# A planner that judges orders by an in-order replay with late transfers: one fused attention and feed-forward kernel

## The chip, the cores and the metric

The kernel runs on one core of a Trainium2 chip. A core has five engines that each execute their own queue of instructions in order: TensorE (PE, matmuls and their weight loads), VectorE (DVE), ScalarE (ACT), GpSimd (POOL) and SyncE (SP), which here only issues DMA transfers. They wait for each other through semaphores. The metric is the device time of the program in microseconds (us); the median of three runs is compared.

## What is computed

A linear attention over 8 batches, 8 heads, 576 positions and 64 dimensions per head, followed by a feed-forward layer over all 4608 tokens (512 to 2048 to 512) in float32:

```python
q_s = q - np.max(q, axis=-1, keepdims=True)
q_s = np.exp(q_s)
q_s = q_s / (np.sum(q_s, axis=-1, keepdims=True) + 1e-09)
k_s = k - np.max(k, axis=2, keepdims=True)
k_s = np.exp(k_s)
k_s = k_s / (np.sum(k_s, axis=2, keepdims=True) + 1e-09)
kv = np.einsum('bhsd,bhse->bhde', k_s, v)
attn = np.einsum('bhsd,bhde->bhse', q_s, kv).astype(np.float32)
...
x = np.ascontiguousarray(attn.transpose(0, 2, 1, 3)).reshape(B * S, H * D)
h = x @ w_in
g = np.where(h >= 1, h, np.where(h <= -1, 0.0, (h + 1) ** 2 / 4.0))
out = (g @ w_out).astype(np.float32)
```

## The kernel before

*Tiling.* The 4608 tokens are cut into nine chunks of 512. A float32 operand is held as two parts (high and low), and a product of two such operands takes three matmuls of 128 x 128 by 512. The first three chunks go one by one: for each of 16 blocks of 128 hidden features there is a first layer (`first_layer`, L1613, tile h), the activation g on ScalarE and VectorE (`middle`), and a second layer into four PSUM banks (`second_layer`, L1822, tile o). The other six chunks go in pairs, three turns: `two_first_layers` (L1671) takes seven products for four blocks (tiles hA, hB, hC, with VectorE additions at L1695 and copies sn), and half of the g blocks of the second chunk are kept in DRAM (`keep`) and read back (`recall`, tile gs). The weights are split on the chip during the first chunk (`weights`, L455 to L497: loads st, shift L467, join L470, split), stored to DRAM and streamed in later (`fetch`, L535, tiles w from b or s). The attention of a chunk (`attention`, `attention_two`, L1215 and after) is spread over the feed-forward work of the chunk before: loads of k, v and q (L1240), a maximum over k (L1252), exponentials, the kv product (L1304), the maximum and sum over q, the product x (L1491), its copy to DRAM (xk, L1527) and back (xc, L1161). A finished output bank is copied by ScalarE or VectorE to osb (L392, L394) and stored (L1880).

*What sets the order.* None of these steps is issued where it stands in the code. Each is an `Op` of a `Plan`, with its engine (sometimes two to choose from), a price in us, a due time, its dependencies (data and the freeing of buffers, by `Ring`), its kilobytes if it is a transfer, and whether it locks the port that VectorE and GpSimd share. `Plan.order` builds a first order by due times. `Plan.settle` then repeats 450 times: `late` (places every step as late as it can, from the end), a random shift of up to eight steps that aren't transfers, near an idle place of PE in the plan, and `early` (places every step as early as it can). A try is kept if the planned end doesn't grow. At the end the steps of all engines are issued sorted by planned start, and that order is each engine's queue.

*How transfers are planned.* A transfer takes 0.45 us of SyncE, then `FIRST` us, then its kilobytes at `KB_PER_US` on a "wire". `early` and `late` put it into any free hole of the SyncE row and of the wire row (`gap`), whatever was placed there before. `save` and `read`, for what the kernel writes to DRAM itself, add a margin of 1.2 us; loads of the inputs (k, v, q, st) and the stores of the output are plain `op`s with a margin of 0.

Of the kernel before, what the change touches and what calls it, by code (L numbers as in the profile page):

```python
# [73 lines left out]
LATE = 8  # L74


START, STEP, LEAD = 24.0, 5.5, 20.0


class Op:  # L80
# [4 lines left out]
    def __init__(self, engine, us, due, emit, deps, port, kb, slack, other=()):  # L85
        self.engine, self.us, self.due, self.emit = engine, us, due, emit
        self.port, self.kb, self.slack = port, kb, slack
        self.ways = ((engine, us, port), *other)
        self.deps, self.users = deps, []
        self.missing = len(deps)  # L90
        self.ready = self.after = 0.0
        self.store = False
        self.margin = 0.0
        for d in deps:
            d.users.append(self)

# [18 lines left out]
class Plan:  # L115
# [1 line left out]

    HOP, FIRST, KB_PER_US = 0.12, 2.6, 310.0  # L120

    UNDER_WAY = 8

    TURNS = 450

    PATIENCE = 0.2

# [24 lines left out]
    def save(self, us, due, emit, deps, kb):  # L152
        op = self.op("SP", us, due, emit, deps, kb=kb)
        op.store = True
        op.margin = self.MARGIN
        return op

    def read(self, us, due, emit, deps, kb):
# [38 lines left out]
    def late(self, order):  # L197

        end = max(op.end for op in order)
        used = {e: [] for e in ("PE", "ACT", "DVE", "POOL", "SP", "port", "wire")}  # L200
        starts = {}
        for op in sorted(order, key=lambda op: (op.start, op.end), reverse=True):
            at = issue = end
            for u in op.users:
                if u.engine == op.engine == "SP" and not op.store:
                    issue = min(issue, starts[u] - 0.45)
                else:
                    at = min(at, starts[u] - self.hop(op, u))
            if op.kb:
                us = op.kb / self.KB_PER_US  # L210
                at = self.gap([used["wire"]], us, at - us - op.margin, True) - self.FIRST
                starts[op] = self.gap([used["SP"]], 0.45, min(at, issue), True)
            else:
                starts[op] = self.fit(op, at - op.us, used, True)
        return starts

    def early(self, starts):

        used = {e: [] for e in ("PE", "ACT", "DVE", "POOL", "SP", "port", "wire")}
        for op in self.ops:  # L220
            op.missing = len(op.deps)
        ready = [(starts[op], op.n, op) for op in self.ops if not op.missing]
        heapify(ready)
        while ready:
            op = heappop(ready)[2]
            for u in op.users:
                u.missing -= 1
                if not u.missing:
                    heappush(ready, (starts[u], u.n, u))
            at = op.after  # L230
            for d in op.deps:
                if d.engine == op.engine == "SP" and not d.store:
                    at = max(at, d.start + 0.45)
                else:
                    at = max(at, d.end + self.hop(d, op))
            if op.kb:
                us = op.kb / self.KB_PER_US
                op.start = self.gap([used["SP"]], 0.45, at)
                op.end = self.gap([used["wire"]], us, op.start + self.FIRST) + us + op.margin
            else:  # L240
                op.start = self.fit(op, at, used, False)
                op.end = op.start + op.us
        return sorted(self.ops, key=lambda op: (op.start, starts[op], op.n))

    def settle(self):


        order, rng = self.order(), random.Random(1)
        for i in range(self.TURNS):
            was = max(op.end for op in order)  # L250
            kept = [(op, op.start, op.end) for op in order]
            starts = self.late(order)
            if i > 1:
                pe = sorted((o.start, o.end) for o in order if o.engine == "PE")
                idle = [(b[0], b[0] - a[1]) for a, b in zip(pe, pe[1:]) if b[0] > a[1] + 0.05]
                about = rng.choices([x for x, _ in idle], [x for _, x in idle])[0]
                about -= rng.uniform(0.0, 8.0)
                near = [o for o in self.ops if o.engine != "SP" and abs(o.start - about) < 6]
                for o in rng.sample(near, min(len(near), rng.choice((1, 2, 4, 8)))):
                    starts[o] += rng.gauss(0.0, 3.0)  # L260
                order = self.early(starts)
                starts = self.late(order)
            order = self.early(starts)
            if max(op.end for op in order) > was + 1e-9:
                for op, op.start, op.end in kept:
                    pass
                order = [k[0] for k in kept]
        return order

    def bias(self, op, engine):  # L270
# [9 lines left out]
    def order(self):  # L280
        self.inherit()
        free = {op.engine: 0.0 for op in self.ops}
        avail = {e: [] for e in free}
        port = wire = 0.0
# [10 lines left out]
        while len(out) < len(self.ops):  # L295
# [32 lines left out]
            if locks:  # L328
                port = end
            if op.kb:  # L330
                end = wire = max(t + self.FIRST, wire) + op.kb / self.KB_PER_US
                landed.append(end)
                end += op.margin
            op.end = end
# [11 lines left out]
def tile_linear_attention_then_ffn(  # L346
# [321 lines left out]
    def attention(c, pr, due, step, slack, kdue=None):  # L668
# [318 lines left out]
        if has_k:  # L987
            if c < KT:
# [7 lines left out]
                rzs.free(kz)  # L996
                rrz.take(kz)
                et = room(f"ps h{pr % 2}", 1) if first else rpk
                tr = do("PE", 0.7, 2, kt_tr, ke, *rpk.wait(), *(et.wait() * first))
                rpk.take(tr)  # L1000
                copies = [("DVE", 0.69, False)], [("ACT", 0.25, False)]
                kc = do("ACT", 0.58, 2.5, kt_copy, tr, *rk.wait(), other=copies[0])
# [62 lines left out]
        qn = do("POOL", 1.04, 3, q_rows("qrz", ALU.mult), qz, port=True)  # L1065
        rqz.free(qn)
        if first:
            tr = do("PE", 0.6, 3.6, q_tr, qn, *rpq.wait())
        elif rows:
            mm = do("PE", 0.95, 3.6, kv_mm, kc, kd, lv, *rpk.wait())  # L1070
            rpk.take(mm)
            rk.free(mm)
            kh = do("ACT", 0.62, 4.2, kv_hi, kz, mm, *parts)
            kl = do("DVE", 0.57, 4.4, kv_lo, kh)
            rpk.free(kl)
            tr = do("PE", 0.6, 3.6, q_tr, qn, *rpq.wait())
        else:
            rqt = room("wk qt", 1)
            tr = do("DVE", 0.71, 3.6, q_blocks, qn, *rqt.wait(), port=True)
            rqt.take(tr)  # L1080
# [134 lines left out]
    def attention_two(c, h, kdue, qdue):  # L1215
# [131 lines left out]
        if c < NB:  # L1347
# [8 lines left out]
                    pr, "v", v[c, pr], [P, KJ, P + 2], 325, kdue + 33 + 3 * i, "v"  # L1356
                )
            for i, pr in enumerate(two):
                km = do("DVE", 0.8, kdue + 6 * i, k_max(i), loads[pr, "k"], *maxed, port=True)
                maxed = [km]  # L1360
                if not i:
                    rm.take(km)
                loads[pr, "m"] = km
# [24 lines left out]
            ra = ring("ps a", 1)  # L1388
            at = kdue + 34
            deps = [loads[pr, "v"] for pr in two]  # L1390
            mm = do("PE", 1.68, at, kv_mms, *exps, *deps, *ra.wait())
            ra.take(mm)
            for pr in two:
                rooms[pr, "k"].free(mm)
# [162 lines left out]
        for i, pr in enumerate(two):  # L1557
# [8 lines left out]
            rql.take(lo)  # L1566
            rqt.free(lo)
            deps = [kvdone.get((c - 1, pr)), kvdone.get((c, pr))]
            xm = do("PE", 0.9, at + 5, x_mm(pr), lo, *[d for d in deps if d], *ra.wait())
            ra.take(xm)  # L1570
            rqh.free(xm)
            rql.free(xm)
# [481 lines left out]
```

## Time and profile before

| | |
|---|---|
| median of three runs | 861.32 us (857.89, 861.32, 863.23) |
| the profiled execution | 863.48 us, of which the span from the first to the last instruction is 861.70 us |
| PE matmuls | 840.2 us busy, 4272 instructions |
| DVE, ACT, POOL | 512.6, 473.5, 301.0 us busy |
| DMA | 166.39 MB in 455 transfers of SyncE, 193 GB/s in the mean |
| longest waits of PE | 3.8, 3.7 and 3.2 us |

Matmuls are pipelined: one of 512 columns is shown with some 390 ns but the next starts after about 227, so the busy time of PE is the union of overlapping pieces, not their sum. A granted clock (PEclk) below 1.00 says that PE ran at half speed for a part of that stretch. In a row of a timeline, what stands in brackets is how long the engine was idle before it and what ended the idle time. The engine named as the end of a wait is the last link: it may itself have stood behind something in its queue.

### The profile page before, as it was taken

What the parts mean: (1) busy time and instruction counts of PE and PEld (TensorE: products, weight loads), DVE (VectorE), ACT (ScalarE), POOL (GpSimd) and SP (SyncE); (2) the same over time, 40 slices, a digit from 0 to 9 for tenths busy, and PEclk for the clock granted to TensorE, in tenths of its full rate; (3) what the DMA queues carried; (4) which work ended last, traced back from release to release, by engine and by line L of the source; (5) the groups of instructions that cost most, each with busy time, mean ns of one, the idle gap of its engine ahead of it and who ended that gap; (6) DMA issues with size and microseconds to landing.
All of it is one profiled execution on the core that took longest, in us unless ns stands there. A gap on an engine that the chain in (4) does not pass through costs nothing. (4 is left out here: it accounts for less than half of the span.)

```text
span 861.7 us, 12255 instructions
## 1 busy us (share of the span) xinstructions
PE 840.2 (97%) x4272; PEld 685.7 (80%) x4272; DVE 512.6 (59%) x956; ACT 473.5 (55%) x834; POOL 301.0 (35%) x270
## 2 busy tenths in 40 slices
PE   8799999999999999999898999999999999999998
PEld 6587788888888887878676888888887888888786
DVE  7887867767766747767577626677652034545300
ACT  7787856455655656555466345556574344445522
POOL 5554565542557253111213162122155810000153
PEclk9999999999999999999999999999999999999999
DMA  8788975257476548557566525566456244544232
GB/s 331 246 295 301 301 243 183 88 196 256 158 273 232 192 150 333 182 179 262 183 195 220 167 92 189 171 218 214 156 170 218 88 152 141 172 159 147 71 113 86
DMA packets 65582, 166.39 MB, mean 193 GB/s; under 512 B 7280, under 2 KB 7536, under 8 KB 65520
## 3 DMA queue, kind: packets, MB, share of 16 engines
q1 hardware_dynamic: 65520, 165.61, 56.9%
q8 instruction: 34, 0.56, 0.3%
q14 instruction: 28, 0.23, 0.1%
HBM read 122.06 MB, written 43.52 MB: 192 GB/s over the span
## 5 line engine op out<-in xcount | busy, mean ns | idle before, releaser
L1822 PE MATMUL o<-wl,gh 128*128 128x512 f32 x576 | 228.3, 396 | 4.0 <-ACT osb L392 3.5
L1822 PE MATMUL o<-wh,gl 128*128 128x512 f32 x576 | 226.0, 392 | 0.1
L1822 PE MATMUL o<-wh,gh 128*128 128x512 f32 x576 | 225.5, 391 | 0.0
L1671 PE MATMUL hA<-x,w 128*128 128x512 f32 x576 | 148.5, 394 | 5.0 <-DVE c L1695 4.8
L1671 PEld LDWEIGHTS hA<-x,w 128*128 128x128 f32 x576 | 107.8, 189 | 29.9 <-DVE c L1695 7.0
L1822 PEld LDWEIGHTS o<-wl,gh 128*128 128x128 f32 x576 | 108.8, 189 | 27.9 <-ACT osb L392 4.8
L1822 PEld LDWEIGHTS o<-wh,gl 128*128 128x128 f32 x576 | 108.8, 189 | 24.9 <-POOL gl L1811 0.9
L1822 PEld LDWEIGHTS o<-wh,gh 128*128 128x128 f32 x576 | 109.1, 189 | 21.6
L1613 PE MATMUL h<-x,w 128*128 128x512 f32 x432 | 110.5, 400 | 5.8 <-DVE gl L1811 4.6
L1613 PEld LDWEIGHTS h<-x,w 128*128 128x128 f32 x432 | 80.7, 190 | 24.6 <-DVE gl L1811 5.2
L1765 ACT ACTIVATE r<-r 128x512 f32<-128x512 f32 x144 | 90.9, 632 | 3.6
L1671 PE MATMUL hC<-x,w 128*128 128x512 f32 x288 | 73.7, 391 | 0.3 <-DVE gl L1811 0.2
L1762 ACT ACTIVATE r<-c,half 128x512 f32<-128x512 f32 x48 | 34.7, 722 | 65.0 <-DVE c L1695 64.7
L1806 ACT CAST gh<-gs 128x512 fp32r<-128x512 f32 x42 | 26.1, 622 | 73.7 <-PE o L1822 62.9
L1671 PEld LDWEIGHTS hC<-x,w 128*128 128x128 f32 x288 | 53.7, 188 | 12.6 <-ACT sn_P L392 0.8
L1436 POOL TENSOR_TENSOR q<-q,qmb 128x512 f32<-128x512 f32 x28 | 30.2, 1097 | 94.1 <-DVE qmb L1428 73.1
L1811 POOL TENSOR_TENSOR gl<-gs,gh 128x512 fp32r<-128x512 f32 x34 | 43.8, 1293 | 49.2 <-ACT gh L1806 49.1
L1762 ACT ACTIVATE r<-h,half 128x512 f32<-128x512 f32 x48 | 32.9, 688 | 47.8 <-PE h L1613 47.6
L1436 POOL TENSOR_TENSOR q<-q,qzb 128x512 f32<-128x512 f32 x28 | 29.8, 1084 | 83.4 <-DVE qzb L1458 74.2
L1768 DVE SCALAR_TENSOR_TENSOR h<-h,r 128x512 f32<-128x512 f32 x48 | 33.1, 693 | 36.3 <-ACT r L1765 36.2
L1193 POOL TENSOR_TENSOR x<-xc,x 128x512 fp32r<-128x512 f32 x30 | 38.9, 1310 | 28.7 <-ACT x L1188 22.6
L1811 POOL TENSOR_TENSOR gl<-c,gh 128x512 fp32r<-128x512 f32 x5 | 6.5, 1304 | 121.2 <-PE o L1822 117.5
(149 smaller groups left out, 1282.7 us busy)
## 6 DMA issues: line engine op xcount, KB each, us to landing
w<-b SPq DMA_DIRECT2D x50, 512.0 KB, 4.9
w<-s SPq DMA_DIRECT2D x48, 512.0 KB, 3.4
st<-in_w SPq DMA_DIRECT2D x32, 512.0 KB, 5.6
g<-c SPq DMA_DIRECT2D x42, 256.0 KB, 3.2
gs<-g SPq DMA_DIRECT2D x42, 256.0 KB, 2.7
v<-in_v SPq DMA_DIRECT2D x32, 325.0 KB, 5.3
q<-in_q SPq DMA_DIRECT2D x36, 256.0 KB, 3.9
out<-osb SPq DMA_DIRECT2D x35, 256.0 KB, 3.1
```

The costliest lines, as they stand in the source:

```text
L1193: eng.tensor_tensor(x[:, 1, :], t["xc"][:, at, :], f32(x[:, 0, :]), ALU.subtract)
L1436: nc.gpsimd.tensor_tensor(qf, qf, at, alu)
L1613: nc.tensor.matmul(t["h"], lhs, rhs, start=(at == 0 and i == 0), stop=(at == NPAIR - 1 and i == 2),)
L1671: nc.tensor.matmul(banks[b]["h"], lhs, rhs, start=(begins and not kk and not m), stop=(ends and kk == 1 and m == 2), skip_group_check=True,)
L1762: nc.scalar.activation(t["r"], t["h"], AF.Relu, bias=half[:, :1], scale=0.5)
L1765: nc.scalar.activation(t["r"], t["r"], AF.Square)
L1768: nc.vector.scalar_tensor_tensor(t["h"], t["h"], 1.0, t["r"], ALU.max, ALU.min)
L1806: nc.scalar.copy(t["gh"], t["h"])
L1811: eng.tensor_tensor(t["gl"], t["h"], f32(t["gh"]), ALU.subtract)
L1822: nc.tensor.matmul(outs[c, j], lhs[:, s], rhs, start=(begins and i == 0), stop=(closes and i == 2),)
```

## The change

Only the planner is changed: no instruction of any engine is added, removed or resized, but their order is a new one.

- A transfer has a `wire` time of its own: KB / 330 for loads, KB / 290 for what `save` writes; 2.05 us come before it instead of 2.6. Every transfer has a margin of at least 0.8 us.
- An order is no longer judged by the planned end but by `play`, a replay in which every engine takes its steps strictly in the given order, SyncE and the wire too. A gap of PE over 3 us (after `START`, 24 us) is charged with 2.4 us more. `cost` is the mean end over three cases, in each of which every transfer lands up to 1.6 us late, by chance.
- `settle` starts from one pass of `late` and `early` over the first order and then makes displacements around the gaps that the replay found. Transfers can now be displaced as well. Every displacement has a number that seeds its random choices; those that were accepted are listed in `TURNS`, and only these are made. Odd numbers get a second pass.
- Prices: the maximum over k of `attention_two` 0.8 to 1.3 us, and six PE prices lower.

```diff
-        self.margin = 0.0
+        self.margin = 0.8 if kb else 0.0
+        self.wire = kb / 330
...
-    HOP, FIRST, KB_PER_US = 0.12, 2.6, 310.0
+    HOP, FIRST = 0.12, 2.05
...
-    TURNS = 450
+    TURNS = (
+        10014, 10015, 10016, 10017, 10018, 10019, 10021, 10022, 10024, 10028, 10029, 10030,
...
+        10853, 10854, 10855, 10859, 10860, 10861, 10862,
+    )
+
+    CASES, LATE = 3, 1.6
...
         op.margin = self.MARGIN
+        op.wire = kb / 290
         return op
...
-                us = op.kb / self.KB_PER_US
+                us = op.wire
...
+    def play(self, order, late):
+
+        free = dict.fromkeys(("PE", "ACT", "DVE", "POOL", "SP", "port", "wire"), 0.0)
+        ends = {}
+        gaps = []
+        for op in order:
+            t = max(free[op.engine], op.after)
+            if op.port:
+                t = max(t, free["port"])
+            for d in op.deps:
+                if d.engine != op.engine:
+                    t = max(t, ends[d] + 0.05)
+                elif d.store or op.engine != "SP":
+                    t = max(t, ends[d])
+            if op.kb:
+                free["SP"] = t + 0.42
+                free["wire"] = max(free["wire"], t + self.FIRST) + op.wire
+                ends[op] = free["wire"] + late[op.n]
+                continue
+            if op.engine == "PE" and t > free["PE"] + 0.1:
+                gaps.append((op.start, t - free["PE"]))
+                if t > free["PE"] + 3 and t > START:
+                    t += 2.4
+            ends[op] = free[op.engine] = t + op.us
+            if op.port:
+                free["port"] = ends[op]
+        return max(ends.values()), gaps
+
+    def cost(self, order):
+        total, self.gaps = 0.0, []
+        for late in self.lates:
+            end, gaps = self.play(order, late)
+            total += end / self.CASES
+            self.gaps += gaps
+        return total
+
     def settle(self):
-        order, rng = self.order(), random.Random(1)
-        for i in range(self.TURNS):
-            was = max(op.end for op in order)
+        rng = random.Random(0)
+        self.lates = [
+            [rng.uniform(0.0, self.LATE) if op.kb else 0.0 for op in self.ops]
+            for _ in range(self.CASES)
+        ]
+        order = self.early(self.late(self.order()))
+        was, gaps = self.cost(order), self.gaps
+        for i in self.TURNS:
+            rng = random.Random(i)
             kept = [(op, op.start, op.end) for op in order]
             starts = self.late(order)
-            if i > 1:
-                pe = sorted((o.start, o.end) for o in order if o.engine == "PE")
-                idle = [(b[0], b[0] - a[1]) for a, b in zip(pe, pe[1:]) if b[0] > a[1] + 0.05]
-                about = rng.choices([x for x, _ in idle], [x for _, x in idle])[0]
-                about -= rng.uniform(0.0, 8.0)
-                near = [o for o in self.ops if o.engine != "SP" and abs(o.start - about) < 6]
-                for o in rng.sample(near, min(len(near), rng.choice((1, 2, 4, 8)))):
-                    starts[o] += rng.gauss(0.0, 3.0)
-                order = self.early(starts)
-                starts = self.late(order)
+            about = rng.choices([x for x, _ in gaps], [x for _, x in gaps])[0]
+            about -= rng.uniform(0.0, 8.0)
+            near = [op for op in self.ops if abs(op.start - about) < 6]
+            for op in rng.sample(near, min(len(near), rng.choice((1, 2, 4, 8)))):
+                starts[op] += rng.gauss(0.0, 3.0)
             order = self.early(starts)
-            if max(op.end for op in order) > was + 1e-9:
+            if i % 2:
+                order = self.early(self.late(order))
+            now = self.cost(order)
+            if now > was + 1e-9:
                 for op, op.start, op.end in kept:
                     pass
                 order = [k[0] for k in kept]
+            else:
+                was, gaps = now, self.gaps
         return order
...
-                tr = do("PE", 0.7, 2, kt_tr, ke, *rpk.wait(), *(et.wait() * first))
+                tr = do("PE", 0.6, 2, kt_tr, ke, *rpk.wait(), *(et.wait() * first))
...
-            tr = do("PE", 0.6, 3.6, q_tr, qn, *rpq.wait())
+            tr = do("PE", 0.45, 3.6, q_tr, qn, *rpq.wait())
...
-            mm = do("PE", 0.95, 3.6, kv_mm, kc, kd, lv, *rpk.wait())
+            mm = do("PE", 0.9, 3.6, kv_mm, kc, kd, lv, *rpk.wait())
...
-                km = do("DVE", 0.8, kdue + 6 * i, k_max(i), loads[pr, "k"], *maxed, port=True)
+                km = do("DVE", 1.3, kdue + 6 * i, k_max(i), loads[pr, "k"], *maxed, port=True)
...
-            mm = do("PE", 1.68, at, kv_mms, *exps, *deps, *ra.wait())
+            mm = do("PE", 1.38, at, kv_mms, *exps, *deps, *ra.wait())
...
-            xm = do("PE", 0.9, at + 5, x_mm(pr), lo, *[d for d in deps if d], *ra.wait())
+            xm = do("PE", 0.8, at + 5, x_mm(pr), lo, *[d for d in deps if d], *ra.wait())
```

More of the change, by code (lines that the diff above doesn't have):

```diff
@@ L236, in early @@
             if op.kb:
-                us = op.kb / self.KB_PER_US
+                us = op.wire
                 op.start = self.gap([used["SP"]], 0.45, at)
@@ L330, in order @@
             if op.kb:
-                end = wire = max(t + self.FIRST, wire) + op.kb / self.KB_PER_US
+                end = wire = max(t + self.FIRST, wire) + op.wire
                 landed.append(end)
@@ L1075, in attention @@
             rpk.free(kl)
-            tr = do("PE", 0.6, 3.6, q_tr, qn, *rpq.wait())
+            tr = do("PE", 0.45, 3.6, q_tr, qn, *rpq.wait())
         else:
```

27 rows, old and new, of the table TURNS are left out of this document.

## Prediction

> **What bounds the kernel now.** I read the page's busy times first, then the granted clock, then busy time and clock by stretch, then the waits of TensorE, and last the order of work around each long wait.
>
> ```profile
> span 861.7 us, 12255 instructions
> ...
> PE 840.2 (97%) x4272; PEld 685.7 (80%) x4272; DVE 512.6 (59%) x956; ACT 473.5 (55%) x834; POOL 301.0 (35%) x270
> ```
>
> ```profile
> core 0: 861.7 us, clock 0.991
> ```
>
> TensorE (PE) is busy for 97% of the span, and the change takes no instruction away from it. Whatever it wins must come out of the 21.5 us in which PE is idle and of the time that PE spends at a lower clock. The view by stretch says where that is (width, then busy us of PE, PEld, DVE, ACT, POOL, then clock, share of the DMA engines, GB/s):
>
> ```profile
> core 0: us, PE busy (x) PEld busy (x) DVE busy (x) ACT busy (x) POOL busy (x), PEclk, DMA share, GB/s
> 0.00:21.00 21.00, 18.08 (x158) 14.15 (x158) 15.60 (x39) 15.36 (x34) 11.18 (x16) 1.00 0.91 339
> 21.00:29.50 8.50, 7.60 (x29) 5.11 (x30) 6.96 (x13) 6.73 (x13) 6.22 (x5) 1.00 0.68 203
> 29.50:38.00 8.50, 4.66 (x15) 3.51 (x14) 8.03 (x16) 5.74 (x10) 4.46 (x4) 0.80 0.87 313
> ...
> 74.00:337.00 263.00, 263.00 (x1477) 216.50 (x1476) 184.93 (x361) 155.39 (x284) 130.22 (x121) 1.00 0.64 220
> ...
> 420.00:431.00 11.00, 7.29 (x26) 5.50 (x25) 6.13 (x9) 3.69 (x6) 3.28 (x3) 0.84 0.69 252
> 431.00:442.00 11.00, 10.88 (x51) 9.01 (x50) 6.82 (x11) 5.25 (x10) 1.43 (x2) 1.00 0.59 192
> 442.00:445.00 3.00, 1.95 (x9) 1.29 (x8) 2.88 (x5) 1.97 (x3) 0.00 (x0) 1.00 0.52 175
> 445.00:468.00 23.00, 23.00 (x138) 18.59 (x137) 18.68 (x38) 17.38 (x31) 9.69 (x8) 1.00 0.57 184
> 468.00:479.00 11.00, 7.79 (x23) 5.91 (x22) 4.58 (x9) 3.61 (x8) 0.72 (x1) 0.69 0.65 239
> 479.00:858.00 379.00, 378.25 (x1737) 310.94 (x1736) 169.89 (x290) 181.66 (x302) 104.10 (x85) 1.00 0.46 151
> ```
>
> From 74 to 337 us PE has no idle time at all, and from 479 to 858 us 0.75 us. The losses sit in four places. Idle (width less PE busy): 8.50 - 4.66 = 3.84 us; 11.00 - 7.29 = 3.71; 3.00 - 1.95 = 1.05; 11.00 - 7.79 = 3.21; together 11.81 us. Clock (one less PEclk, times the width): 0.20 x 8.5 = 1.7 us; 0.16 x 11 = 1.76; 0.31 x 11 = 3.4, of which about 0.6 fell into the idle time itself (half clock from 471.02, PE back at 472.25, by rows further down), so 2.8. Together 6.26 us. **These four places cost 18.07 us, and that is what a better order can win**, next to nothing else.
>
> PE's waits name who ended the long ones (total, times, longest):
>
> ```profile
> PE hA L1671 <- DVE c L1695: 4.8, 2, 3.7
> PE h L1613 <- DVE gl L1811: 4.6, 2, 3.8
> PE o L1822 <- ACT osb L392: 3.5, 2, 3.2
> ```
>
> The engine named is only the last link. The order of work on VectorE and SyncE around 421 us:
>
> ```profile
> 423.12 1.25 DVE L1252 TENSOR_REDUCE m<-k 128x128 f32<-128x640 f32 x1 [4.04 <-DMA k<-in_k]
> 424.40 0.69 DVE L1695 TENSOR_TENSOR c<-hC,sn_P 128x512 f32<-128x512 f32 x1
> 425.01 0.68 DVE L1695 TENSOR_TENSOR c<-hA,sn_P 128x512 f32<-128x512 f32 x1
> ```
>
> ```profile
> 409.50 7.53 SPq L535 DMA_DIRECT2D w<-s  x2
> ...
> 418.03 0.94 SPq L1240 DMA_DIRECT2D k<-in_k  x2
> ```
>
> ```profile
> DMA to landing us min/median/max: 5.1/5.6/6.0
> ```
>
> SyncE sat behind two weight fetches until 417 us; the loads of k went out at 418.03 and, with the v loads behind them, took 5.1 to 6.0 us to land (last row). VectorE executes in order: the reduction of k stood first, waited 4.04 us, and the two additions that PE needed stood behind it. At 442 us the same happens behind a q load (first row below). At 469 us ScalarE stands in front of a copy whose buffer a store has not given back:
>
> ```profile
> 441.63 0.69 DVE L1416 TENSOR_REDUCE qa<-q 128x16 f32<-128x512 f32 x1 [2.38 <-DMA q<-in_q]
> ...
> 471.61 0.59 ACT L392 COPY osb<-o 128x512 f32<-128x512 f32 x1 [2.78 <-DMA out<-osb]
> ...
> 472.25 0.79 PE L1822 MATMUL o<-wl,gh 128*128 128x512 f32 x1 [3.21 <-ACT osb L392]
> ```
>
> ```profile
> DMA to landing us min/median/max: 3.1/5.5/5.8
> ```
>
> The last row is for the three stores of osb there: 5.5 us in the median, 3.1 at best. So three of the four losses are one pattern: a transfer queued behind others lands later than the plan had it, and an in-order engine stands on it in front of work that PE needs. All three transfers (k, q, out) are plain ones, which the old plan gives a margin of 0.
>
> **The change part by part.** *Instructions.* Nothing is added or removed on any engine and no DMA changes its size: each of PE's 4272 matmuls keeps its own duration. What changes is the order, on every queue, SyncE's and GpSimd's included. The direct cost is 0.
>
> *Margins and the queue model (margin 0.8 for every transfer, 2.05 us to the first byte, 330 KB/us for loads and 290 for stores, replay in issue order).* For the k loads the replay gives, alone, 2.05 + 320/330 = 3.0 us and two transfers later 5.0; the trace has 5.1 to 6.0, inside the 1.6 us of lateness that it draws. So the replay sees the stall at 421 us that the old plan, which fitted a transfer into any free hole of the wire, could not. Gain: 3.71 + 1.76 = 5.47 us. The q load at 442 us: 1.05 us. The store at 469 us, likewise in range: 3.21 + 2.8 = 6.0 us. Sum of the three 12.5 us. What is late next there: PE itself, since the rows from 431 and from 445 us show 0.12 us and no idle time.
>
> *The price of the k reduction (0.8 to 1.3).*
>
> ```profile
> L1252 DVE TENSOR_REDUCE m<-k x24: 1212/1305/1341, 122.9 to 517.0; 128x128 f32<-128x640 f32 x24
> ```
>
> 24 x 0.5 us = 12 us of VectorE work that the plan did not know. VectorE is 59% busy, so it costs nothing now; knowing it removes half a microsecond of surprise per reduction, counted within the 12.5. The lower PE prices (q_tr 0.45, kv_mms 1.38, x_mm 0.8) alter the plan alone. Should one be too low, PE is merely later than planned, which gives the other engines time: 0.
>
> *The replay's charge of 2.4 us for PE gaps above 3 us, and displacements that may now pick transfers.* These aim the search at the three longest losses. The one at the start, at 30 us, is of another kind:
>
> ```profile
> 27.44 1.39 DVE L467 TENSOR_SCALAR st<-st 128x512 uint32<-128x512 uint32 x1 [1.28 <-DMA st<-in_w]
> ...
> 29.95 0.68 DVE L1768 SCALAR_TENSOR_TENSOR h<-h,r 128x512 f32<-128x512 f32 x1
> ...
> 30.80 1.56 DVE L467 TENSOR_SCALAR st<-st 128x512 uint32<-128x512 uint32 x1
> ...
> 32.88 0.68 DVE L1811 TENSOR_TENSOR gl<-h,gh 128x512 fp32r<-128x512 f32 x1
> ```
>
> PE waits for gl, which ends at 33.56. VectorE is busy for 8.03 of those 8.5 us, and L467, priced 0.52, takes 1.39 and 1.56. A better order can put h and gl ahead of the weight work, but the work stays. Bounds: 0 (nothing won) to 3.84 + 1.7 = 5.54 (all). I take 3.5, nearer the top, since a gap cut below 2 us also saves the half clock, and keep 2.0.
>
> *New stalls.* Another order can create waits that the trace does not show. Bounds: 0, and 12.5 us (a second set like the three above). I take 1.0, near the 0.75 us of the stretch from 479 us, which holds the same kind of work.
>
> **Sum.** 12.5 + 3.5 - 1.0 = 15.0 us. The profiled execution took 863.48 us (span 861.7); 863.48 - 15.0 = **848.5 us**. It is 2.2 us above the median of 861.32, so against the median the gain is 12.8 us, 1.5%. All four places cured gives 863.48 - 18.07 = 845.4.
>
> [...] The clock around the two late gaps, in stretches of 3.41 us:
>
> ```profile
> 419.83:423.24 3.41, 1.61 (x8) 0.99 (x6) 0.12 (x1) 0.00 (x0) 1.48 (x2) 1.00 0.98 364
> 423.24:426.65 3.41, 1.50 (x7) 1.24 (x8) 3.14 (x5) 1.49 (x3) 1.80 (x2) 1.00 0.78 304
> ...
> 467.61:471.02 3.41, 1.43 (x7) 0.85 (x5) 2.54 (x7) 1.18 (x3) 0.00 (x0) 1.00 0.99 343
> 471.02:474.43 3.41, 2.18 (x5) 1.80 (x6) 1.40 (x2) 2.21 (x4) 0.00 (x0) 0.50 0.84 322
> ```
>
> A stretch with PE busy for 1.43 us (idle 1.98) is followed by a clock of 0.50; one with 1.61 us busy (idle 1.80) is not. So a gap of 3.21 us was enough. [...]
>
> **The rivals.**
> - *Lateness beyond the model.* The replay draws at most 1.6 us. Two v loads issued from 463.9 us landed after 5.5 to 5.8 us, where 2.05 us and the bytes of v and of the k ahead give 4.0: 1.5 to 1.8 late. If the store at 469 us and the start stay as they are, only 5.47 + 1.05 are won: 857.0 us. For it: the DMA engines are at 0.98 and 0.99 in both late stalls. Against: the margin of 0.8 also moves transfers ahead.
> - *Stalls just below the charge.* The replay charges the clock only above 3 us idle, while the trace shows half clock after 1.98 us idle in a stretch. Two gaps of 2.5 us, each with 1.7 us of half clock, give 848.5 + 8.4 = 856.9 us. [...]
> - *The change does not do what it says.* The losses only move to other places, as the order is new everywhere and the old plan also took its own gaps for small: 859 to 866 us, about 862.
> - *Slower.* The stretch from 479 us works through the next pair of chunks with the same loads of k and q and nearly no idle time. If transfers moved closer to their use repeat the pattern there, that pair pays the same 12.5 us while the first is not cured: 863.48 + 12.5 = 876 us. With the first places cured as in the sum it would be 863.48 - 15.0 + 12.5 = 861.0, no change; so it decides once the new losses are larger than what is won before 479 us, and is slower by 1% from about 9 us net above the median. SyncE's long waits in that stretch (longest 5.6 us in the rows below) speak for it, the 0.46 share of the DMA engines against.
>
> ```profile
> SPq L535 <- PE hA L1671: 79.7, 32, 5.6
> SPq L1792 <- POOL gl L1811: 59.5, 26, 5.6
> ```
>
> **How the numbers follow.** Forecast 0.62 (own range 844 to 853), lateness 0.13, stalls below the charge 0.06, only moved 0.12, slower 0.07. The range reaches from 844 (all cured, and a microsecond of the 2.9 us idle before 21 us) up to 860, which takes in the two rivals at 857: 0.81 and a little of the next. A measurement of this kernel can tell about 1% from no change: faster is below 852.7 us, 0.60, nearly all of the forecast; within 1% 0.33; slower 0.07.
>
> **What would show it.** Right: PE busy about 840 again with a span near 847; the clock nearer 1.00 than 0.991; no PE wait for c (L1695) or osb (L392) above 1 us; k reductions that wait for no transfer, or with nothing behind them that PE needs; at 30 us a gap below 2 us. Wrong: a row of PE waits of 2 to 4 us in a new place, above all after 479 us, or a clock of 0.99 or less with the gaps still above 3 us.

## The result and the profile after

| | before | after |
|---|---|---|
| median | 860.75 us (6 runs) | 852.22 us (6 runs, 850.47 to 853.50) |
| ratio, with its 95% interval | | 0.9904 [0.9879, 0.9929] |
| the profiled execution | 863.48 us | 853.50 us |

One of the six runs of the kernel before took 1045.53 us; it counts in the median but not in the ratio, and without it the median is 860.18 us. The change made the kernel faster by 1.0%. The forecast of 848.5 us was 3.7 us too low; the time lies in the range of 844 to 860. The forecast was worked out from the profiled execution, where 15.0 us were to be won and 10.0 came. When the changed kernel was run again on another chip (e7 below) it took 850.72 us, ratio 0.9879 [0.9855, 0.9904].

First the span and busy times of the changed kernel's page, then its granted clock, then its busy time by stretch with the columns as before:

```profile
span 851.7 us, 12257 instructions
...
PE 835.9 (98%) x4272; PEld 682.0 (80%) x4272; DVE 525.6 (62%) x976; ACT 474.0 (56%) x829; POOL 288.3 (34%) x255
```

```profile
core 0: 851.7 us, clock 0.998
```

```profile
0.00:21.00 21.00, 17.00 (x158) 13.15 (x158) 15.28 (x43) 14.16 (x29) 12.55 (x17) 1.00 0.91 338
...
29.50:38.00 8.50, 7.16 (x46) 5.19 (x45) 6.85 (x15) 7.09 (x14) 4.54 (x5) 1.00 0.99 332
...
68.00:73.00 5.00, 3.97 (x17) 2.65 (x16) 4.34 (x7) 3.44 (x8) 3.62 (x3) 1.00 0.95 346
...
337.00:370.00 33.00, 32.06 (x137) 24.63 (x137) 22.21 (x39) 17.26 (x29) 3.84 (x5) 1.00 0.53 169
...
415.00:426.00 11.00, 9.06 (x34) 6.98 (x33) 6.07 (x11) 3.82 (x8) 1.70 (x2) 0.84 0.76 272
426.00:479.00 53.00, 52.78 (x268) 42.69 (x266) 37.41 (x63) 34.61 (x61) 8.55 (x8) 1.00 0.60 199
479.00:847.60 368.60, 367.74 (x1691) 302.45 (x1689) 171.93 (x298) 178.04 (x296) 96.48 (x77) 1.00 0.47 153
```

PE's idle time (span less PE busy) fell from 21.5 to 15.8 us, by 5.7, and the clock losses of the four places named before from 6.26 to 1.76 us (0.16 x 11, the row from 415 us), by 4.5. Together that is 10.2 us, against 10.0 by the spans. Place by place:

| place | forecast | measured |
|---|---|---|
| 421 us (after: 415 to 426) | -5.47 | -1.77: 1.94 idle and 1.76 of clock are left |
| 442 and 469 us (after: 426 to 479) | -7.05 | -6.83: 0.22 idle is left, the clock is 1.00 |
| the start, 29.5 to 38 us | -3.5 | -4.2: 1.34 idle is left, the clock is 1.00 |
| new stalls | +1.0 | about +2.7: 1.08 more before 21 us, 0.41 more from 38 to 74, 0.53 more from 337 to 370, 0.4 more after PE's last matmul, 0.3 in small pieces |

The idle times at 68 us (1.03) and after 337 us (0.94) in the rows above are only partly new: the kernel before has 0.78 us from 38 to 74 and 0.41 us from 337 to 370. One long gap remained where the sum had none. The waits of PE, with their total, count and longest:

```profile
PE o L1898 <- DVE gl L1887: 3.7, 3, 1.9
PE h L1689 <- DVE gl L1887: 1.2, 3, 0.8
```

All lines of the changed kernel are shifted: gl is L1887, the additions of `two_first_layers` L1771, the k load L1316, its maximum L1328, the fetch L611. PE waits for osb for 0.4 us at most, and its longest wait is 1.9 us instead of 3.8. That wait has the old shape. SyncE, VectorE and PE of the changed kernel, in order of time:

```profile
413.48 0.32 SPq L611 DMA_DIRECT2D w<-s  x1
413.89 0.38 SPq L1603 DMA_DIRECT2D xk<-xo  x1
414.32 0.97 SPq L1316 DMA_DIRECT2D k<-in_k  x2
```

```profile
418.71 1.23 DVE L1328 TENSOR_REDUCE m<-k 128x128 f32<-128x640 f32 x1 [4.36 <-DMA k<-in_k]
419.86 0.68 DVE L1887 TENSOR_TENSOR gl<-hb,gh 128x512 fp32r<-128x512 f32 x1
420.46 0.68 DVE L1771 TENSOR_TENSOR c<-hC,sn_P 128x512 f32<-128x512 f32 x1
```

```profile
411.90 1.54 PE L1747 MATMUL hC<-x,w 128*128 128x512 f32 x6
...
420.59 0.50 PE L1898 MATMUL o<-wh,gl 128*128 128x512 f32 x1 [1.94 <-DVE gl L1887]
```

Again the maximum over k waits over 4 us for its load, with gl behind it. But the k load isn't late by chance. It stands behind a weight fetch in SyncE's queue, and SyncE stood on that fetch until the matmuls of hC had ended: 411.90 + 1.54 = 413.44, the fetch went out at 413.48. SyncE's long waits in this stretch, from 400 to 425 us, name the same matmuls:

```profile
SPq L611 <- PE hC L1747: 7.4, 2, 5.6
```

The kernel does have to wait there, but its planner does not know it. A weight buffer of `two_first_layers` serves two products (the first and second in order, the third and fourth, the fifth and sixth; the seventh is alone), and the plan frees it with one of them:

```python
        for mm_ in (p2, p6, p7, p4):
            rws.free(mm_)
```

The fourth product, p6, depends on p1 and a copy, not on the third, p5 (tile hC). So the planner may put p5 after p6, and then takes the buffer for free while p5 still has to read it. The replay inherits what is missing: in four draws of lateness it gives PE gaps of at most 0.6 us there for the changed order, where the chip has 1.94, and at most 1.8 us in sum for the order before, where the chip has 3.71.

### The profile page after: what moved, and what is told of

It is laid out like the page before. It is cut to its first block, busy times and chain, and to the rows that moved or that the text cites. A ratio compares the mean times of both kernels' runs of the same rounds, so it can differ in the third digit from the quotient of the medians.

```text
span 851.7 us, 12257 instructions
## 1 busy us (share of the span) xinstructions
PE 835.9 (98%) x4272; PEld 682.0 (80%) x4272; DVE 525.6 (62%) x976; ACT 474.0 (56%) x829; POOL 288.3 (34%) x255
## 4 chain that ended last, share of the span: by engine, by line
PE 89%; DVE 5%; DMA 3%; ACT 2%; issue 1%; POOL 1%; SPq 0%; POOLq 0%; ACTq 0%; DVEq 0%
PE o L1898 43%; PE hA L1747 15%; PE h L1689 13%; PE hC L1747 8%; PE hb L1747 4%; PE x L1567 2%; PE kv L1380 2%; DMA st<-in_w 1%; DMA q<-in_q 1%; DVE gl L1887 1%; DMA v<-in_v 1%; PE x L1033 0%; DVE qzo L1503 0%; DVE st L546 0%; ACT r L1838 0%
## 5 line engine op out<-in xcount | busy, mean ns | idle before, releaser
L1689 PE MATMUL h<-x,w 128*128 128x512 f32 x432 | 107.6, 393 | 0.2 <-DVE gl L1887 0.2
L1887 POOL TENSOR_TENSOR gl<-gs,gh 128x512 fp32r<-128x512 f32 x30 | 38.7, 1291 | 30.4 <-ACT gh L1882 30.1
L1887 POOL TENSOR_TENSOR gl<-c,gh 128x512 fp32r<-128x512 f32 x4 | 5.2, 1290 | 124.2 <-ACT gh L1882 124.1
L1882 ACT CAST gh<-h 128x512 fp32r<-128x512 f32 x48 | 28.1, 587 | 26.7 <-DVE h L1844 13.9
```

The source lines that it names most:

```text
L1689: nc.tensor.matmul(t["h"], lhs, rhs, start=(at == 0 and i == 0), stop=(at == NPAIR - 1 and i == 2),)
L1882: nc.scalar.copy(t["gh"], t["h"])
L1887: eng.tensor_tensor(t["gl"], t["h"], f32(t["gh"]), ALU.subtract)
```

## The experiments

**Which part of the change wins.** e1 to e4 ran beside the kernel before on one chip. e1 keeps everything but the displacements: it issues the order of one `late` and `early` pass.

```diff
-    TURNS = (
-        10014, 10015, 10016, 10017, 10018, 10019, 10021, 10022, 10024, 10028, 10029, 10030,
...
-    )
+    TURNS = ()
```

> The changed planner with its margins, prices and one pass of late and early, but with no displacement at all. Theory (an order is won by the displacements that the replay accepts; the planner's own replay ends at 857.5 us for the order before and 848.8 for the changed one, and the chip took 3.3 us more in both): this order's replay ends at 858.7, so 862 us, as before or 1 us worse. Rival (the new margins and transfer constants alone do it): about 852 to 854 us, as the changed kernel.

Measured: 856.07 us, 0.9927 [0.9905, 0.9949]. The expectation failed by 6 us: this order, judged by nothing, is already faster than the kernel before. Its 0.7% is most of the 1.0% of the changed kernel. The stretch from 410 to 482 us holds all three late losses. First this stretch in the kernel before, the changed one, e1 and e2 (below), then the start in e1:

```profile
410.00:482.00 72.00, 63.91 (x333) 51.06 (x332) 47.49 (x91) 38.56 (x70) 15.76 (x15) 0.93 0.57 191
410.00:482.00 72.00, 69.85 (x368) 56.44 (x365) 50.27 (x94) 41.40 (x74) 12.06 (x11) 0.98 0.58 195
410.00:482.00 72.00, 71.86 (x386) 58.27 (x386) 52.41 (x100) 44.13 (x78) 13.44 (x13) 1.00 0.67 220
410.00:482.00 72.00, 65.03 (x298) 51.78 (x297) 45.93 (x82) 37.69 (x67) 13.26 (x12) 0.91 0.54 177
```

```profile
29.50:41.00 11.50, 6.65 (x21) 4.85 (x20) 8.76 (x17) 7.22 (x13) 6.46 (x6) 0.70 0.92 318
```

In e1 PE is idle for only 0.14 us of these 72 us, at full clock. **One pass of the changed planner cured all three late places without any replay**, 421 us included; the changed kernel, with its displacements, has 2.15 us of idle time there. What e1 lacks is the start: PE is busy for 6.65 of 11.50 us at a clock of 0.70, and the displacements of the changed kernel cure that (10.00 us busy in the same stretch, at 1.00). e1 has the new margins, rates and prices and leaves out the 450 old tries, both at once. The old planner without its tries was not run, so whether the margins are needed for this is open.

e2 keeps the new rates, margins and prices, and takes the old `settle`: 450 tries judged by the planned end.

```diff
+    TURNS = 450
...
+        order, rng = self.order(), random.Random(1)
+        for i in range(self.TURNS):
+            was = max(op.end for op in order)
...
+            if max(op.end for op in order) > was + 1e-9:
```

> The new margins, transfer rates and prices, but the old way of judging: 450 displacements, kept if the planned end does not grow; no replay. Theory (the judging in issue order with lateness is what wins): replay of this order 863.2 us, so 866 us, slower than before by some 0.6%. Rival (the transfer model wins): 852 to 855 us.

Measured: 863.70 us, 1.002 [1.0000, 1.0041]. So with the new model of transfers but the old judging nothing is won. e1 and e2 differ only in the 450 tries and what judges them: **these displacements, judged by the planned end, cost 7.6 us** (863.70 - 856.07), and the stalls from 410 to 482 us are back (fourth row above). That they shorten a plan whose transfers fit into holes that the queue does not have is a likely reason, which no run shows by itself.

e3 judges by the replay, without lateness, with 850 displacements of its own, and issues the 20 that were accepted.

```diff
-    CASES, LATE = 3, 1.6
+    CASES, LATE = 1, 0.0
```

> The changed planner with a replay in issue order but no lateness (one case, LATE 0), and 850 fresh displacements judged by it. Replay without lateness 847.3 us (the order before 847.1, the changed one 842.7), with lateness 857.1. Theory (lateness in the judging is needed): 860.5 us, as before. Rival (issue order alone is enough): 854 us or less.

Measured: 861.24 us, 0.9998 [0.9974, 1.0021]. In this one search an in-order replay with exact transfers is no better than the old judging: its displacements lose the 5.2 us that e1 has without any. e3 leaves out the lateness, but its displacements are others too, so that lateness alone makes the difference is not shown.

e4 keeps the changed planner and takes another 850 displacements, of which 130 were accepted (its `TURNS` lists those).

> The changed planner as it is, but with 850 other displacements (130 of them accepted) than those listed. Replay with lateness 850.6 us, 1.8 above the changed kernel's. Theory (the replay's end tells the chip's time but for a constant of about 3.3 us): 854 us. Rival (the listed displacements fit the chip and the replay is not what carries it): 857 to 862 us.

Measured: 855.32 us, 0.9919 [0.9891, 0.9946]. That is e1's time within what can be told (0.9927), so these displacements kept what the single pass had and won nothing measurable over it. The listed ones won some 2 to 4 us over e1 (0.9904, and 0.9879 in e7, against 0.9927); the first of these two intervals overlaps e1's.

`play` of the changed planner, averaged over twelve draws of lateness for each of these orders, shows how far it can be trusted (the expectations name its values for the planner's own three draws):

| order | replay | chip | chip less replay |
|---|---|---|---|
| before | 857.4 | 860.75 | 3.4 |
| after | 847.8 | 852.22 | 4.4 |
| e1 | 858.1 | 856.07 | -2.0 |
| e2 | 862.4 | 863.70 | 1.3 |
| e3 | 856.3 | 861.24 | 4.9 |
| e4 | 850.0 | 855.32 | 5.3 |
| e8 (below) | 840.8 | 848.26 | 7.5 |

The runs come from several chips, on which the kernel before took 860.66 to 861.86 us in the comparisons of e1 to e8. The replay puts e1 0.7 us behind the order before, and on e1's chip it was 5.8 us ahead (861.86 - 856.07); differences of that size it cannot rank. An order chosen because the replay liked it (after, e3, e4, e8) comes out 4.4 to 7.5 us above the replay, one that was not (before, e1, e2) between 2.0 below and 3.4 above: the choosing also finds the places where the replay is too kind. The widest miss is not in the table: e10 (below) came out 11.3 us above its own replay of 844.2, which has a stricter charge and one more dependency.

**What stands at 420 us.** e5 takes the kernel before and moves one step: the maximum over k (2107) behind the two additions that PE needs (1730 is the second).

```diff
     order = plan.settle()
+    one, other = plan.ops[2107], plan.ops[1730]
+    order.remove(one)
+    order.insert(order.index(other) + 1, one)
```

> The order before with a single step moved on VectorE: the reduction of k that waited for its load at 421 us goes behind the two additions that PE needed. Theory (that one queue position cost 3.7 us of idle time and 1.7 us of half clock): 5 us faster than before, a ratio of 0.994. Rival 1 (the wait only moves to the next step that needs the load): no change, which is also what the replay of the changed planner says of this move (857.8 against 857.5). Rival 2 (the clock is not part of it): 3.5 us, 0.996.

Measured: 856.98 us, 0.9955 [0.9936, 0.9973]. VectorE and the stretch from 420 us in e5:

```profile
421.50 0.69 DVE L1695 TENSOR_TENSOR c<-hC,sn_P 128x512 f32<-128x512 f32 x1 [0.35 <-PE hC L1671]
422.11 0.68 DVE L1695 TENSOR_TENSOR c<-hA,sn_P 128x512 f32<-128x512 f32 x1
425.01 1.32 DVE L1252 TENSOR_REDUCE m<-k 128x128 f32<-128x640 f32 x1 [2.23 <-DMA k<-in_k]
```

```profile
420.00:431.00 11.00, 11.00 (x50) 9.05 (x49) 7.80 (x13) 6.43 (x12) 3.31 (x3) 1.00 0.98 328
```

The maximum still waits 2.23 us for its load, and nobody waits for it: PE is busy for all 11.00 us at a clock of 1.00, where before it was 7.29 at 0.84. The cause of this stall is shown, and its price: 0.45% is 3.9 us, against 5.47 us in the sum; the interval, 2.3 to 5.5 us, just reaches it. In e5's profile the clock at the start was 0.70 from 29.5 to 41 us, so its profiled execution, 859.34 us, isn't a measure of the gain.

e6 does the same in the changed kernel: the maximum over k and the GpSimd step behind it go after gl and the additions.

```diff
     order = plan.settle()
+    pair, other = [plan.ops[2107], plan.ops[2109]], plan.ops[1730]
+    order = [o for o in order if o not in pair]
+    at = order.index(other) + 1
+    order[at:at] = pair
```

> The changed order with the same reduction of k (and the GpSimd step that follows it) moved behind the three VectorE steps that PE needed at 420 us. Theory (the 1.94 us gap left there and its half clock are caused by this position): 3.6 us faster than the changed kernel, 848.5 us. Rival (the replay is right on this move): 2 us slower than the changed kernel, 854 us.

Measured: 849.74 us, 0.9874 [0.9852, 0.9897]. e7 is the changed kernel itself on that chip.

> The changed kernel once more, unedited, on the chip of this comparison: 852 us, ratio 0.990 to the kernel before. It is the yardstick for the two beside it.

Measured: 850.72 us, 0.9879 [0.9855, 0.9904]. e6 is 1.0 us better than e7, within what can be told; the gap moved to a step behind, 0.9 us of it. That is 4 us below the 854 us which the replay had for this move, so the replay is wrong here; how much the position cost, the test does not tell, as e7's own profile has no half clock (1.000 in the mean).

e9 leaves VectorE alone and takes the wait out of SyncE's queue: the fetch (1760) is issued behind the k and v loads (2106 is the last) instead of before them.

```diff
     order = plan.settle()
+    fetch_, last = plan.ops[1760], plan.ops[2106]
+    order.remove(fetch_)
+    order.insert(order.index(last) + 1, fetch_)
```

> The changed order with one transfer moved on SyncE: the weight fetch that waited until 413.5 us goes behind the store of x and the loads of k and v that stood behind it. Theory (the fetch waits for a product hC of which the plan does not know, and holds the k loads up for 2 to 3 us): the k loads go out near 411 us, the reduction of k hardly waits, the PE gap of 1.9 to 2.1 us at 420 us is gone, and the fetch itself goes out no later; 2 us faster than the changed kernel (with half clock in some executions 3.6), 849 us, ratio 0.987. Rival (the k loads are held by the bandwidth, or by their buffers, not by the fetch): no change, 851 to 852 us, and a wait of the k reduction of 4 us as before.

Measured: 849.49 us, 0.9862 [0.9834, 0.9889]. SyncE, VectorE and the stretch around it in e9:

```profile
409.27 0.92 SPq L1316 DMA_DIRECT2D k<-in_k  x2
410.24 0.90 SPq L1316 DMA_DIRECT2D v<-in_v  x2
412.12 0.33 SPq L611 DMA_DIRECT2D w<-s  x1
```

```profile
413.02 1.22 DVE L1328 TENSOR_REDUCE m<-k 128x128 f32<-128x640 f32 x1
414.16 0.68 DVE L1887 TENSOR_TENSOR gl<-hb,gh 128x512 fp32r<-128x512 f32 x1
```

```profile
405.00:426.00 21.00, 20.86 (x128) 16.97 (x127) 17.41 (x38) 11.76 (x23) 5.49 (x6) 1.00 0.78 253
```

The k loads go out 5 us earlier (409.27 against 414.32). Of these, 1.35 us come from e9 being ahead as a whole, by the same matmuls of hC (at 410.55 against 411.90), so 3.7 us come from the move. The maximum waits for nothing, gl follows at once, and 0.14 us of idle time is left of the 1.94, at full clock. The fetch itself is no later: it goes out at 412.12, when hC has ended (410.55 + 1.54 = 412.09). So the stall of the changed kernel hung on a fetch that stood in front of the loads and waited for a product that the plan had left out. Against e7, on another chip, the medians differ by 1.2 us, with overlapping intervals; the size is measured better by the next pair.

**A better order.** e8 starts from the changed kernel's order and takes some 70,000 single moves of steps, judged by `play` over six cases of lateness with a charge of 1.7 us for every gap above 1.6 us; the whole sequence is then written out.

```diff
-    order = plan.settle()
+    plan.order()
+    order = [plan.ops[n] for n in SEQUENCE]
```

> The changed planner's order, refined by some 70000 single moves in the queues, judged by the same replay over six cases of lateness, with the clock charged (1.7 us) for every gap above 1.6 us. Replay with that charge: 840.6 us over fresh cases, where the changed order has 849.8. Theory (the replay's end carries over to the chip, and what the change left was a search that had stopped early): 9 us faster than the changed kernel, about 843 to 845 us, with PE idle next to nothing after 24 us. Rival (the replay is too coarse below some 5 us, so a finer order only fits its errors): 848 to 853 us.

Measured: 848.26 us, 0.9851 [0.9827, 0.9875]. On the same chip that is 2.5 us below e7, where 9 were expected; it lies in the range of the rival, a replay too coarse for a finer order. The stall is again at the same place. e12 is e8 with the fetch moved behind the first k load.

```diff
     order = [plan.ops[n] for n in SEQUENCE]
+    fetch_, first = plan.ops[1760], plan.ops[2103]
+    order.remove(fetch_)
+    order.insert(order.index(first) + 1, fetch_)
```

> The refined order of the second comparison (848.3 us, with a PE gap of 2.8 us and half clock at 418 us) with one transfer moved: the weight fetch that SyncE held until its product hC was done goes behind the first k load. Theory (the same unknown wait as in the changed order, the k load 3.5 us late for it): the k load goes out near 408.5 us, the gap and its half clock are gone, 4 us faster than the refined order, about 844 us, ratio 0.980; the fetch goes out no later. Rival (the reduction of k meets the next late thing, as in the two orders of the third comparison): 848 us, with a gap of 2 us or more in a new place between 410 and 500 us.

Measured: 843.59 us, 0.9782 [0.9757, 0.9808], the best of all kernels here and 2.2% faster than before. SyncE, VectorE and the stretch from 400 us, in e8:

```profile
412.01 0.32 SPq L793 DMA_DIRECT2D w<-s  x1
412.38 0.42 SPq L1498 DMA_DIRECT2D k<-in_k  x1
```

```profile
416.75 1.23 DVE L1510 TENSOR_REDUCE m<-k 128x128 f32<-128x640 f32 x1 [4.89 <-DMA k<-in_k]
417.90 0.68 DVE L2069 TENSOR_TENSOR gl<-hb,gh 128x512 fp32r<-128x512 f32 x1
```

```profile
400.00:430.00 30.00, 27.19 (x147) 21.63 (x146) 21.64 (x45) 14.86 (x27) 6.24 (x6) 0.94 0.67 225
```

and the same in e12:

```profile
408.48 0.33 SPq L1498 DMA_DIRECT2D k<-in_k  x1
412.72 0.32 SPq L793 DMA_DIRECT2D w<-s  x1
```

```profile
412.12 1.24 DVE L1510 TENSOR_REDUCE m<-k 128x128 f32<-128x640 f32 x1
413.83 0.69 DVE L2069 TENSOR_TENSOR gl<-hb,gh 128x512 fp32r<-128x512 f32 x1 [0.48 <-ACT gh L2064]
```

```profile
400.00:430.00 30.00, 30.00 (x169) 24.78 (x169) 24.72 (x50) 18.04 (x33) 6.18 (x6) 1.00 0.73 246
```

Of 30 us, PE is busy for 27.19 at 0.94 in e8 and for 30.00 at 1.00 in e12: 2.81 + 0.06 x 30 = 4.6 us. The two ratios differ by 0.69%, 5.9 us, and their intervals do not touch. **In this order one transfer, moved by one place past one k load, is worth 0.7%; the whole change is worth 1.0 to 1.2%.**

e10 and e11 give the planner the missing dependency instead.

```diff
-        for mm_ in (p2, p6, p7, p4):
-            rws.free(mm_)
+        for used in ((p1, p2), (p5, p6), (p3, p7), (p4,)):
+            rws.free(*used)
```

e10 also takes an order refined by the replay under that rule, as in e8; e11 changes these lines alone, with the displacements of `TURNS` retried.

> As the refined order of the second comparison, but the planner now counts a weight buffer as free only when both products that read it are done (before, by the second one named alone). Replay with that rule and the stricter clock charge: 844.2 us over fresh cases, where the changed planner's own search has 854.5. Theory (this missing dependency is what the refined order still paid for, with its gap of 2.8 us and half clock at 418 us): no PE gap above 1 us after 35 us, 844 to 846 us, ratio 0.981, 3 us faster than the refined order. Rival (residual lateness that no plan foresees): 848 us as before.

> The changed planner with that dependency alone added; the listed displacements are tried again on it, so the order is a new one. Replay by the corrected rule 854.3 us, where the changed order has 856.6 (engine by engine). Theory (the dependency was what the replay lacked): 849 to 850 us, 2 us faster than the changed kernel. Rival (the listed displacements were found on the other model, and fewer of them are accepted now): 852 to 856 us.

Measured: e10 855.49 us, 0.9924 [0.9895, 0.9952]; e11 858.56 us, 0.9975 [0.9959, 0.9991]. Both missed, by about 10 us. No wait is left at 420 us, but there are new ones, in e11 one of 3.4 us at the start and one of 4.8 us at 478 us. PE and GpSimd in e11:

```profile
477.83 0.79 PE L1898 MATMUL o<-wh,gl 128*128 128x512 f32 x1 [4.76 <-POOL gl L1887]
```

```profile
457.35 1.29 POOL L1887 TENSOR_TENSOR gl<-c,gh 128x512 fp32r<-128x512 f32 x1 [4.93 <-DVE gl L1887]
465.15 0.72 POOL L1356 PARTITION_ALL_REDUCE m<-m  x1 [6.50 <-issue]
475.50 1.04 POOL L1512 TENSOR_TENSOR q<-q,qzb 128x512 f32<-128x512 f32 x1 [9.63 <-issue]
476.51 1.26 POOL L1887 TENSOR_TENSOR gl<-gs,gh 128x512 fp32r<-128x512 f32 x1
```

The gl that PE needs stood in GpSimd's queue behind the maximum across partitions (PARTITION_ALL_REDUCE) and one step after it. From the end of the step before the maximum to the start of the step after it, 458.64 to 475.50, are 16.9 us; the plan prices the maximum at 13.6. In the changed kernel the same stretch is 14.2 us, from 451.32 (450.02 + 1.30) to 465.50, and there the profile puts the last part down to a step x of VectorE:

```profile
450.02 1.30 POOL L1269 TENSOR_TENSOR x<-xc,x 128x512 fp32r<-128x512 f32 x1 [1.29 <-ACT x L1264]
457.68 0.77 POOL L1356 PARTITION_ALL_REDUCE m<-m  x1 [6.36 <-DVE gl L1887]
465.50 2.06 POOL L1512 TENSOR_TENSOR q<-q,qmb 128x512 f32<-128x512 f32 x2 [7.05 <-DVE x L1269]
```

In e10 a gl behind the same kind of step made PE wait 3.7 us at 492 us, and its clock was 0.86 from 0 to 24 us, with a gap of 2.6 us at 12 us; the replay charges nothing for a gap before 24 us. Both orders are new everywhere, so they met other weak places of the model. That a planner with the right dependency and a better price for this step would do better was not tried, and why it is 14.2 us in one order and 16.9 in another stays open.

## Why the prediction was right, and which step failed

- **Sign and size.** Idle time and clock losses together went down at all four places, though by far the least at 421 us. The reason given, in-order judging with late transfers, holds only in part. One unjudged pass (e1) already wins 0.7% and cures the three late places; the replay was not needed for them. That was not foreseen. The old tries themselves did harm (e2), and the search without lateness (e3) did as well. What the judging with lateness added to the pass is 2 to 4 us with the listed displacements and nothing measurable with others (e4). So the size, inside the range, came in part by another way than the one forecast.
- **The failed step: "So the replay sees the stall at 421 us".** It sees less than half of it. The step took the k loads as late by queueing behind other transfers, inside the replay's draw of 1.6 us. The runs showed SyncE standing on a weight fetch, for a product that the plan's release rule leaves out, in the kernel before and after alike. That made the k loads 3.7 us late (e9 against the changed kernel, measured from the matmuls of hC), and no draw of the replay reaches that. The term was 5.47 us and 1.77 came. Of the 5.0 us that the profiled execution fell short by, 3.7 are missing here and 1.7 went to more new stalls than forecast; that the median, too, lies 3.7 us above the forecast is a coincidence. The rows for it were quoted in the prediction (SyncE behind two weight fetches until 417 us); the question that was not asked is what the fetch itself waited for, and whether the plan knows it.
- **442 and 469 us.** 7.05 us forecast, 6.83 measured. The step is right in its result. e1 shows that the replay was not needed for it, and e2 that the new margins do not keep it when the old tries follow.
- **The start.** 3.5 us forecast, 4.2 measured: 1.34 us of idle time is left, and the clock is 1.00. This is the place where the displacements earn their keep, since e1 has 4.85 us of idle time at a clock of 0.70 from 29.5 to 41 us.
- **New stalls.** 1.0 us forecast, about 2.7 measured; the row from 479 us, which the size was taken from, is 0.86 against 0.75, but the first 74 us without the start gave 1.6.
- **The rivals.** "Stalls just below the charge" came in part: one gap of 1.94 us with half clock. It was not the charge that let it through, since the replay has 0.6 us at most there. "Lateness beyond the model" had 421 us cured and 469 us and the start not; the chip did the opposite. Nothing moved into the stretch after 479 us, so the slower rival did not occur.

**The clock.** In the changed kernel the half clock after the gap lies in one stretch of 3.41 us. First the stretch ahead of it and this one, then two stretches around the gap in e7, the same program:

```profile
417.63:421.05 3.42, 1.49 (x7) 0.94 (x6) 2.34 (x3) 0.00 (x0) 0.00 (x0) 1.00 1.04 403
421.05:424.46 3.41, 3.41 (x10) 2.64 (x9) 3.07 (x7) 2.60 (x4) 0.47 (x1) 0.50 0.48 163
```

```profile
417.02:420.43 3.41, 2.00 (x9) 1.31 (x7) 1.24 (x2) 0.00 (x0) 0.00 (x0) 1.00 1.04 408
420.43:423.85 3.42, 2.77 (x12) 2.32 (x13) 3.18 (x6) 2.13 (x4) 0.00 (x0) 1.00 0.61 213
```

```profile
421.08 0.50 PE L1898 MATMUL o<-wh,gl 128*128 128x512 f32 x1 [2.06 <-DVE gl L1887]
```

In the changed kernel the gap of 1.94 us lies within the first of these stretches, which leaves PE busy for 1.49 of 3.42 us, and in the next the clock was 0.50. In e7 a longer gap, 2.06 us, lies across the two stretches shown (2.00 and 2.77 us busy), and the clock was 1.00 in both and 1.000 in the mean of the execution. So the same order paid 1.7 us (half of 3.41) of half clock in one execution and none in the other, after the longer gap. That it depends on where the gap falls is a guess from these two: no run shows it, and e7's clock, which did not change there, marks no borders of stretches. The prediction's hope that a gap below 2 us saves the half clock did not hold for the 1.94 us here, and no run shows a limit at 2 us.

## What to carry to other kernels

Run the order that nobody judged beside the judged ones: here one pass with margins had most of the gain, 450 tries judged by an exact plan lost it again, and a replay in issue order with random lateness added 0 to 4 us to it. Before trusting such a replay, take each long wait of the issuing engine in the trace and look for it among the planner's dependencies: one buffer freed by one of its two readers left the replay with 0.6 us where the chip had a gap of 1.94. Adding the dependency is not enough by itself, since a new order meets other gaps of the model (e10, e11). On SyncE a fetch that had to wait held up the loads behind it, by 3.7 us in the changed kernel (e9), so put the transfers that wait for nothing ahead of it.

## What was not expected of the hardware

- A clock of 0.50 for 3.41 us after a gap of only 1.94 us in the changed kernel, and a clock of 1.00 after one of 2.06 us in e7, as shown above.
- Around the maximum across partitions GpSimd ran nothing else for 14.2 us in the changed kernel and 16.9 in e11, while the instruction itself shows 0.77 and 0.72 us. Most of the difference lies behind it: 7.05 us until the next instruction in the changed kernel, 9.63 in e11.
